# Linear attention and a Strassen feed-forward block: score products as 64x64 quarters, regrouped attention stages, and a fixed TensorE order

## The chip, the cores and the metric

The kernel runs on one core of one Trainium2 chip. The metric is the device time of one execution in microseconds (us). Before the change three runs gave 666.48, 668.00 and 668.18 us, with a median of 668.0 us.

A core has a matrix engine (TensorE, "PE" in the profile, with its weight loads listed as "PEld"), VectorE ("DVE"), ScalarE ("ACT"), GpSimd ("POOL") and SyncE ("SP"). Each engine works through its own queue of instructions in order, and waits at the head of it on semaphores of the others. DMAs are started here from the queues of SP and POOL. TensorE reads SBUF and writes PSUM, which has 8 banks of 128x512 floats.

## The reference

```
# lightning attention, per batch entry and head, blocks of 64 rows, state starts at 0
intra = (q_b k_b^T * lam^(i-j) for i >= j) v_b
inter = (q_b * lam^(i+1)) state
out_b = intra + inter
state = lam^64 * state + (k_b * lam^(63-i))^T v_b
# the heads side by side are the rows x (3072 x 512) of the feed-forward block
h = x @ w_in            # 512 x 2048
y = (h - tanh(h)) @ w_out   # 2048 x 512
```

There are 4 batch entries, 8 heads, 768 positions and 64 columns per head. All is in float32. The size of a block is free in the mathematics, and the kernel uses 128 rows.

## The kernel before

**Groups and chunks.** A group `g` (0 to 5) is 128 positions of all four batch entries, 512 rows of `x`. A chunk `(g, b)` is the part of one batch entry. The four chunks of a group are handled as two halves, `(0, 1)` and `(2, 3)`.

**Attention of a chunk.** `att_transpose` brings q and k into the layout with the head columns on partitions (for g of 2 and more with VectorE transposes of tiles `q_blk` and `k_blk`), and multiplies q by the powers of lam (`qd`). `att_scores` makes the scores: 8 matmuls of 64 contraction rows and 128 output partitions, two heads at a time on the two row halves of the array, into two banks `sp`, each of which VectorE multiplies with the decay mask (`ss`). `att_out` adds, per half, the products of the state with `qd` (L400, 64x64 quarters of the array) and of `v` with `ss` (L406, two column halves of 64) in two banks `op`, which ScalarE copies to `xt`. `att_state` decays k on VectorE (`att_decay`, L361), makes the products of k and v (L374, bank `kv`, two column halves) and updates the state with two VectorE instructions (L379, L380). `att_sums` then makes the sums of `xt` that the feed-forward block needs.

**Feed-forward.** Both products use Strassen's scheme of seven products, in the form named 1, 2, 6, 5, 7, 3, 4, with sums made by VectorE. The up projection (`up`, L458) goes through four column parts `u`. For g of 2 and more its products 2 and 4 are split a second time (`inner_steps`, L542), and so are most products of the down projection (`down_twice`, L686; a plain one is `down`, L633). A partial product stays in a PSUM bank `y`, is copied by ScalarE after each product that completes a quarter, and the next product is added to it in the same bank.

**PSUM.** Four banks have the tag `att`; the other four, `ya`, `yb`, `z` and `w`, belong to the feed-forward block, one buffer each. The bank `y` of an up projection is `ya` for even `u` and `yb` for odd `u`. Both calls of `inner_steps` use `yb` for their `y` (L542), and the ScalarE copies out of it are L546.

**Order.** While the feed-forward block of group g runs, the attention of group g+1 is laid between its products: transposes of `(0, 1)` in part u=2 of the up projection, their scores in u=3, their output and state after the down product 2; then transposes, scores, and output with state of `(2, 3)` after the twice split down products 4, 5 and 6. After the down projection come the products 3 of group g and `inner_steps` 2 of group g+1 in turn, then `inner_steps` 4 mixed with the first up products. Python code gives this program order, but the scheduler of the framework may exchange instructions of an engine by its own estimate, except where `tc.keep_in_program_order` (or `tied` with a true first argument) forbids it. Most matmuls of the feed-forward block and of the attention for g over 0 are free in this sense.

**Loads.** `k_nat` and `v_nat` tiles (256 KB) and the blocks `q_blk`, `k_blk` are loaded by DMAs from the SP queue in a fixed order; k has 3 buffers, v has 4, and the blocks have 7. The tiles `wb` of the feed-forward weights come through POOL, 7 ahead.

Of the kernel before, what the change touches and what calls it, by code (L numbers as in the profile page):

```python
# [24 lines left out]
def kernel(  # L25
# [91 lines left out]
    lam_blk = fwd[:, :, BLK - 1:BLK][:, None, :, :].to_broadcast([128, 2, NP, D])  # L117

# [8 lines left out]
    def load_natural(g, b, names):  # L127
        for name, src, bufs in (("q", q, 2), ("k", k, 3), ("v", v, 4)):
            if name in names:
                x = (qpool if name == "q" else io).tile([128, H, D], F32, name=f"{name}_nat", tag=name, bufs=bufs)  # L130
                op = nc.sync.dma_start(out=x, in_=src[b, :, ts(g, BLK), :].rearrange("h s d -> s h d"))
                tc.keep_in_program_order(op)
                raw[g, b][name] = x
# [189 lines left out]
    def att_transpose(g, bs):  # L323
        for b in bs:
            load(g * B + b + 1)
            t = raw[g, b]
            qt = work.tile([128, NP, BLK], F32, name="qt", tag="qt")
            kt = work.tile([128, NP, BLK], F32, name="kt", tag="kt")
            for dst, x in ((qt, "q"), (kt, "k")):
                if g >= GB:  # L330
                    tc.keep_in_program_order(nc.vector.transpose(out=dst.rearrange("d p i -> d (p i)"),
                                                                 in_=t[x + "b"].rearrange("d p r a -> d (p r a)")))
                else:
                    tp = bank("tp", "att", 4).rearrange("d (p s) -> d p s", p=NP)
                    for p in range(NP):
                        tied(g == 0 or p == 0, nc.tensor.transpose(out=tp[:, p, :], in_=t[x][:, 2 * p:2 * p + 2, :],
                                                                   identity=ident))
                    tied(g == 0, nc.scalar.activation(dst, tp, AF.Copy))
            qd = None
            if g > 0:  # L340
                qd = work.tile([128, NP, BLK], F32, name="qd", tag="qd")
                nc.vector.tensor_tensor(qd, qt, fwd, op=AL.mult)
            tr[g, b] = (qt, kt, qd)

    def att_scores(g, bs):
        for b in bs:
            qt, kt, _ = tr[g, b]

            sp = [bank("sp", "att", 4).rearrange("s (p i) -> s p i", p=NP) for _ in range(2)]
            for p in range(NP):  # L350
                for j in range(2):
                    tied(g == 0, nc.tensor.matmul(out=sp[j][:, p, :], lhsT=kt[ts(j, 64), p, :],  # L352
                                                  rhs=qt[ts(j, 64), p, :], start=True, stop=True))
            ss = work.tile([128, 2, NP, BLK], F32, name="ss", tag="ss")
            for j in range(2):
                tied(g == 0, nc.vector.tensor_tensor(ss[:, j], sp[j], mask[:, j], op=AL.mult))  # L356
            sc[g, b] = ss
# [4 lines left out]

    def att_state(g, bs):
        if g == NG - 1:
            return

        kv = bank("kv", "att", 4).rearrange("d (b p e) -> d b p e", b=2, p=NP)
        for n, b in enumerate(bs):
            kd, vn = raw[g, b]["k"], raw[g, b]["v"]
            if g > 0:  # L370
                att_decay(g, b)
            for p in range(NP):
                for j in range(2):
                    tied(g == 0, nc.tensor.matmul(out=kv[ts(j, 64), n, p, :], lhsT=kd[:, 2 * p + j, :],  # L374
                                                  rhs=vn[:, 2 * p + j, :], start=n == 0 and p == 0, stop=True,
                                                  skip_group_check=True))
        st = state[:, bs[0]:bs[0] + 2]
        if g > 0:
            nc.vector.tensor_tensor(st, st, lam_blk, op=AL.mult)  # L379
            nc.vector.tensor_tensor(st, st, kv, op=AL.add)  # L380
        else:
            tied(True, nc.scalar.activation(st, kv, AF.Copy))

    def att_out(g, bs):
# [3 lines left out]
        ops = [bank("op", "att", 4).rearrange("d (p b s) -> d p b s", p=2, b=2) for _ in range(2)]  # L388
# [5 lines left out]
        if g > 0:  # L394
            for n, b in enumerate(bs):
                for p in (0, 1):
                    for j in range(2):
                        r = ts(j, 64)
                        for pp in (p, p + 2):
                            nc.tensor.matmul(out=dst(n, pp, j), lhsT=state[r, b, pp, :], rhs=tr[g, b][2][r, pp, :],  # L400
                                             start=n == 0 and p == 0, stop=False, skip_group_check=True)
        for n, b in enumerate(bs):
            ss, vn = sc.pop((g, b)), raw[g, b]["v"]
            for p in range(NP):
                for j in range(2):
                    tied(g == 0, nc.tensor.matmul(out=dst(n, p, j), lhsT=vn[:, 2 * p + j, :], rhs=ss[:, j, p, :],  # L406
# [42 lines left out]
    def up(g, u, n):  # L449
# [6 lines left out]
        for m in range(2):  # L456
            for kt in range(2):
                nc.tensor.matmul(out=t[:, m, :], lhsT=wt[:, kt, ts(m, 128)], rhs=x[:, kt, :],  # L458
                                 start=first and m == 0 and kt == 0, stop=kt == 1, skip_group_check=True)
# [4 lines left out]
        def finish(c, src):  # L464
            th = work.tile([128, 2, HB], F32, name="th", tag="th")
            nc.scalar.activation(th, src, AF.Tanh)  # L466
# [6 lines left out]
        elif g >= GI and n == 5:  # L473
            nc.scalar.activation(dst(22), z, AF.Copy)
# [10 lines left out]
        elif n == 6:  # L485
            nc.scalar.activation(dst(12), y, AF.Copy)
# [43 lines left out]
    def inner_steps(g, n, tag):  # L530
# [4 lines left out]
        for x in STEPS:  # L535
# [3 lines left out]
            for u in range(NU):  # L539
                a = wb.rearrange("p m c -> p (m c)")[:, ts(u, 128)] if wb is not None else a_quarter(  # L540
                    n, u, *{1: (0, 0), 2: (0, 1), 7: (1, 0), 4: (1, 1)}[x])
                nc.tensor.matmul(out=dst[:, ts(u, 128)], lhsT=a, rhs=b, start=x in (1, 2, 5) and u == 0, stop=True,  # L542
                                 skip_group_check=True)
            d = dst.rearrange("q (u c) -> q u c", u=NU)
            if x in (1, 4, 6):
                nc.scalar.activation({1: c11, 4: c21, 6: c12}[x], d, AF.Copy)  # L546
            elif x == 5:
                nc.scalar.activation(r5, dst, AF.Copy)
# [73 lines left out]
    def down(g, n):  # L622
# [6 lines left out]
        for u in range(NU):  # L629
            wb = piece(g, n, u)  # L630
            for m in range(2):
                for kt in range(2):
                    nc.tensor.matmul(out=t[:, m, :], lhsT=a[:, u, kt, ts(m, 128)], rhs=wb[:, kt, :],  # L633
                                     start=first and u == 0 and m == 0 and kt == 0, stop=u == NU - 1 and kt == 1,
                                     skip_group_check=True)
# [3 lines left out]
        if n == 1:  # L639
            res[g, 1] = otile("q1")  # L640
            nc.scalar.activation(res[g, 1], t, AF.Copy)
        elif n == 4:
            res[g, 4] = otile("q4")
            nc.scalar.activation(res[g, 4], t, AF.Copy)
# [30 lines left out]
    def down_twice(g, n, zw):  # L675
# [5 lines left out]
        for x, a, dst, keep in ((1, a11, y, o[:, 0:128]), (2, a12, zw[:, 0:128], None), (6, s2, y, o[:, 128:256]),  # L681
# [3 lines left out]
            for u in range(NU):  # L685
                nc.tensor.matmul(out=dst, lhsT=a[:, u, :], rhs=wb[:, ts(u, 128)], start=x in (1, 2) and u == 0,  # L686
                                 stop=u == NU - 1, skip_group_check=True)
            if keep is not None:
                nc.scalar.activation(keep, dst, AF.Copy)  # L689
# [189 lines left out]
    up(1, 0, 1)  # L879
    for g in range(1, NG):  # L880
        last = g == NG - 1
        p0, p1 = attention(g + 1) if not last else ([], [])
        for u in range(NU):
            for n in (2, 6, 5, 7, 1, 4, 3) if g < GI else (1, 7, 3) if u == 0 else (6, 5, 1, 7, 3) if u + 1 < NU else (
# [7 lines left out]
                if g == 1 and u < 2 and n == 5:  # L892
                    sums_in(u + 2)
            if g == GI - 1:
                inner_weights(u)
            if not last and u > 1:
                run(p0[u - 2:u - 1])
        if twice(g, 4):
            sums_twice(g, 4)
        every(down(g, 2))  # L900
        run(p0[2:])
        sums_twice(g, 5)
        every(down_twice(g, 4, "z") if twice(g, 4) else down(g, 4))
        run(p1[0:1])
        sums_once(g, 21, 21, 11)
        sums_twice(g, 6)
        every(down_twice(g, 5, "w"))
        run(p1[1:2])
# [5 lines left out]
        run(p1[2:])  # L914
# [12 lines left out]
        for n in (None, None, 1, None, None, 6, None, None, 5, None):  # L927
            if n is None:
                next(p4)
            else:  # L930
                up(g + 1, 0, n)
        every(p4)
# [30 lines left out]
```

## Time and profile before

| | |
|---|---|
| median of three runs | 668.0 us (666.48 to 668.18) |
| time of the profiled execution | 667.48 us |
| its span from the first to the last instruction | 665.7 us |
| TensorE busy | 653.7 us, 98% |
| VectorE busy | 480.1 us, 72% |
| ScalarE busy | 214.8 us, 32% |
| GpSimd busy | 196.4 us, 30% |
| mean granted TensorE clock | 1.000 |

A float32 matmul leaves two records on TensorE, so a product of 4 matmuls is listed as x8. In a timeline, the first column is the start of a run of like instructions, the second is the time from the start of its first to the end of its last one. Since matmuls are pipelined, the end lies some 0.17 to 0.27 us behind the point at which the next one starts, and the cost of a run is best read as the difference of two starts.

### The profile page before, as it was taken

The page shows a single profiled execution, that of the slowest core. Times are in us where ns is not written, and L with a number is a line of the kernel's source. Part 1 is how long each engine was busy: PE and PEld are TensorE (multiplying, and loading weights), DVE is VectorE, ACT ScalarE, POOL GpSimd, SP SyncE. Part 2 cuts the span into 40 slices and gives each one's busy share as a digit, 9 for nine tenths or more (in the row PEclk, how much of TensorE's full clock was granted, in tenths as well). Part 3 has the DMA queues.
Part 4 walks back from the last instruction along what each step waited for, and adds up shares of the span by engine and source line. Part 5 has one row for each costly group of instructions (what it writes and reads, how often), then busy time and mean ns, then how long its engine had stood idle before and what let it go on. Part 6 is the DMA issues. An engine that isn't in the chain of part 4 may idle for free.

```text
span 665.7 us, 13244 instructions
## 1 busy us (share of the span) xinstructions
PE 653.7 (98%) x4992; PEld 594.6 (89%) x4992; DVE 480.1 (72%) x869; ACT 214.8 (32%) x413; POOL 196.4 (30%) x340
## 2 busy tenths in 40 slices
PE   8899999999999999999999999999999999999988
PEld 7788888888888999888999988999988899988987
DVE  4468897997778983489895378896378787357743
ACT  4788923423321113341112343112333112334110
POOL 0001415783122444001435101345200255300351
PEclk9999999999999999999999999999999999999999
DMA  9999936997345979426889533798721677600584
GB/s 215 226 205 272 294 124 221 347 323 215 79 91 147 294 219 268 88 52 133 233 236 288 132 73 87 182 291 252 202 50 37 156 239 237 205 16 1 141 278 167
DMA packets 158959, 121.76 MB, mean 183 GB/s; under 512 B 133872, under 2 KB 135024, under 8 KB 158896
## 3 DMA queue, kind: packets, MB, share of 16 engines
q0 software_dynamic: 26400, 86.27, 40.7%
q1 hardware_dynamic: 132352, 34.64, 25.6%
q8 instruction: 40, 0.66, 0.4%
q14 instruction: 23, 0.19, 0.1%
q10 hardware_dynamic: 144, 0.00, 0.0%
HBM read 100.67 MB, written 20.19 MB: 182 GB/s over the span
## 4 chain that ended last, share of the span: by engine, by line
PE 76%; issue 9%; DVE 5%; DMA 5%; POOL 2%; ACT 2%; SPq 1%; POOLq 0%; DVEq 0%; ACTq 0%
PE y L458 14%; PE y L686 11%; PE z L458 8%; PE zw L686 8%; PE h L741 7%; PE w L633 4%; PE y L633 4%; PE y L542 3%; PE sp L352 3%; PE op L406 3%; PE acc L771 2%; PE z L542 2%; PE op L400 1%; PE end L725 1%; DMA fine<-wt 1%
## 5 line engine op out<-in xcount | busy, mean ns | idle before, releaser
L598 POOL DMA_DIRECT2D wb<-fine x168 | 90.8, 540 | 138.0 <-PE y L686 59.8
L466 ACT ACTIVATE th<-g 128x512 f32<-128x512 f32 x76 | 47.6, 630 | 99.6 <-DVE g L471 34.2
L689 ACT ACTIVATE q<-y 128x128 f32<-128x128 f32 x96 | 26.7, 278 | 150.3 <-PE y L686 149.5
L458 PE MATMUL y<-xt,w 128*128 128x256 f32 x320 | 73.5, 380 | 0.0
L601 POOL DMA_DIRECT2D wb<-factors x44 | 23.9, 544 | 165.1 <-PE y L633 127.8
L458 PEld LDWEIGHTS y<-xt,w 128*128 128x128 f32 x320 | 59.9, 190 | 8.5 <-ACT g L546 0.9
L467 DVE TENSOR_TENSOR g<-g,th 128x512 f32<-128x512 f32 x76 | 52.1, 689 | 21.1 <-ACT th L466 21.0
L686 PE MATMUL y<-wb,g 128*128 128x128 f32 x456 | 60.6, 278 | 0.0
L741 PE MATMUL h<-xt,w 128*128 128x256 f32 x256 | 58.0, 383 | 1.5 <-DVE w L296 1.4
L686 PEld LDWEIGHTS y<-wb,g 128*128 128x128 f32 x456 | 55.1, 192 | 1.3 <-issue 0.3
L741 PEld LDWEIGHTS h<-xt,w 128*128 128x128 f32 x256 | 47.7, 190 | 9.4 <-DVE w L296 2.1
L686 PE MATMUL zw<-wb,g 128*128 128x128 f32 x304 | 40.3, 275 | 0.1
L458 PE MATMUL z<-tt,ws 128*128 128x256 f32 x160 | 38.1, 381 | 0.0
L458 PE MATMUL y<-tt,ws 128*128 128x256 f32 x160 | 37.8, 379 | 0.0
L458 PE MATMUL z<-xt,ws 128*128 128x256 f32 x160 | 37.8, 379 | 0.0
L686 PEld LDWEIGHTS zw<-wb,g 128*128 128x128 f32 x304 | 37.0, 192 | 0.2 <-DVE g L691 0.2
L633 PE MATMUL w<-wb,g 128*128 128x256 f32 x160 | 35.8, 382 | 0.0
L633 PE MATMUL y<-wb,g 128*128 128x256 f32 x160 | 35.4, 379 | 0.0
L356 DVE TENSOR_TENSOR ss<-sp,mask 128x512 f32<-128x512 f32 x48 | 31.1, 683 | 5.8 <-PE sp L352 5.8
L633 PEld LDWEIGHTS y<-wb,g 128*128 128x128 f32 x160 | 30.4, 190 | 4.1
L458 PEld LDWEIGHTS z<-xt,ws 128*128 128x128 f32 x160 | 30.4, 190 | 4.1
L633 PEld LDWEIGHTS w<-wb,g 128*128 128x128 f32 x160 | 30.1, 190 | 4.4
(178 smaller groups left out, 1292.9 us busy)
## 6 DMA issues: line engine op xcount, KB each, us to landing
wb<-fine POOLq DMA_DIRECT2D x168, 256.0 KB, 4.0
wb<-factors POOLq DMA_DIRECT2D x44, 256.0 KB, 4.3
v_nat<-in_v_dram SPq DMA_DIRECT2D x24, 256.0 KB, 4.8
wb<-fine_in POOLq DMA_DIRECT2D x24, 256.0 KB, 4.3
k_nat<-in_k_dram SPq DMA_DIRECT2D x20, 256.0 KB, 4.9
raw<-in_moe_w_out_dram POOLq DMA_DIRECT2D x10, 512.0 KB, 4.9
raw<-in_moe_w_in_dram SPq DMA_DIRECT2D x8, 512.0 KB, 5.7
raw<-in_moe_w_in_dram SPq DMA_DIRECT2D x16, 256.0 KB, 5.9
```

Of the source, the lines that this page charges most:

```text
L352: tied(g == 0, nc.tensor.matmul(out=sp[j][:, p, :], lhsT=kt[ts(j, 64), p, :], rhs=qt[ts(j, 64), p, :], start=True, stop=True))
L356: tied(g == 0, nc.vector.tensor_tensor(ss[:, j], sp[j], mask[:, j], op=AL.mult))
L458: nc.tensor.matmul(out=t[:, m, :], lhsT=wt[:, kt, ts(m, 128)], rhs=x[:, kt, :], start=first and m == 0 and kt == 0, stop=kt == 1, skip_gro ...
L466: nc.scalar.activation(th, src, AF.Tanh)
L467: nc.vector.tensor_tensor(dst(c), src, th, op=AL.subtract)
L542: nc.tensor.matmul(out=dst[:, ts(u, 128)], lhsT=a, rhs=b, start=x in (1, 2, 5) and u == 0, stop=True, skip_group_check=True)
L598: nc.gpsimd.dma_start(out=t.rearrange("p m c -> p (m c)"), in_=fine[TWICE.index(n_), SUB.index(x_)].rearrange("p u c -> p (u c)"))
L601: nc.gpsimd.dma_start(out=t, in_=factors[XAT[FACT[n_][1]]][:, 2 * x_:2 * x_ + 2, :])
L633: nc.tensor.matmul(out=t[:, m, :], lhsT=a[:, u, kt, ts(m, 128)], rhs=wb[:, kt, :], start=first and u == 0 and m == 0 and kt == 0, stop=u = ...
L686: nc.tensor.matmul(out=dst, lhsT=a[:, u, :], rhs=wb[:, ts(u, 128)], start=x in (1, 2) and u == 0, stop=u == NU - 1, skip_group_check=True)
L689: nc.scalar.activation(keep, dst, AF.Copy)
L741: tied(u == 0, nc.tensor.matmul(out=hm[c][:, m, :], lhsT=w1[u][:, i, a, ts(m, 128)], rhs=xt[0, t][:, i, :], start=m == 0 and i == 0, stop= ...
```

## The change

Nine things change, all for the attention of g from 2 on unless another group is named, and for the order of instructions:

1. The score matmuls are cut into two output halves, so that each one is a 64x64 quarter of the array (L352 before, L359 after): 16 matmuls a chunk instead of 8.
2. The transposes of chunks `(0, 1)` of group g+2 are made while group g+1 starts its up projection; those of `(2, 3)` of g+1 at the end of part u=3. Their scores follow in this order: those of `(0, 1)` at the end of u=2, those of `(2, 3)` after the down product 2, directly ahead of the output of `(0, 1)`. The attention of group 2, which runs beside group 1, keeps the old places for transposes and scores.
3. The output of `(2, 3)` and the state products of all four chunks follow after the twice split down product 6.
4. The output of `(0, 1)` uses the banks `yb` and `w` for groups over 2.
5. The decay of k goes from VectorE (one 128x512 instruction a chunk) to ScalarE (8 instructions of 128x64 a chunk, `decay_steps`), placed between the feed-forward products.
6. The state update is one `scalar_tensor_tensor` for each pair of heads (four of 128x128 a half) instead of two instructions of 128x512 a half; this holds from group 1 on.
7. `qd` of `(2, 3)` is made after the output of `(0, 1)` for groups over 2.
8. The k tile of chunk 3 has a buffer of its own (`k4`).
9. Nearly all matmuls, and most ScalarE copies, are kept in program order.

```diff
+                if name == "k" and b == 3 and g >= GB:
+                    x = late["pool"].tile([128, H, D], F32, name="k_nat", tag="k4", bufs=1)
...
-            qd = None
-            if g > 0:
-                qd = work.tile([128, NP, BLK], F32, name="qd", tag="qd")
-                nc.vector.tensor_tensor(qd, qt, fwd, op=AL.mult)
-            tr[g, b] = (qt, kt, qd)
+            tr[g, b] = (qt, kt)
+            if g > 0 and (g <= GB or b < 2):
+                att_query(g, (b,))
...
+            part = 64 if g >= GB else 128
             for p in range(NP):
                 for j in range(2):
-                    tied(g == 0, nc.tensor.matmul(out=sp[j][:, p, :], lhsT=kt[ts(j, 64), p, :],
-                                                  rhs=qt[ts(j, 64), p, :], start=True, stop=True))
+                    for r in range(128 // part):
+                        tied(g != 1, nc.tensor.matmul(out=sp[j][ts(r, part), p, :], lhsT=kt[ts(j, 64), p, ts(r, part)],
+                                                      rhs=qt[ts(j, 64), p, :], start=True, stop=True))
...
+    def decay_steps(g, b):
+        x = raw[g, b]["k"]
+        for h in range(H):
+            tied(True, nc.scalar.activation(x[:, h, :], x[:, h, :], AF.Copy, scale=mask[:, h % 2, h // 2, BLK - 1:BLK]))
+            yield
...
-            nc.vector.tensor_tensor(st, st, lam_blk, op=AL.mult)
-            nc.vector.tensor_tensor(st, st, kv, op=AL.add)
+            for p in range(NP):
+                nc.vector.scalar_tensor_tensor(out=st[:, :, p, :], in0=st[:, :, p, :], scalar=fwd[:, p, BLK - 1:BLK],
+                                               in1=kv[:, :, p, :], op0=AL.mult, op1=AL.add)
...
-        ops = [bank("op", "att", 4).rearrange("d (p b s) -> d p b s", p=2, b=2) for _ in range(2)]
+        tags = (("yb", 1), ("w", 1)) if g > GB and half == 0 else (("att", 4),) * 2
+        ops = [bank("op", *tag).rearrange("d (p b s) -> d p b s", p=2, b=2) for tag in tags]
...
# up (and likewise down, down_twice, inner_steps; their ScalarE copies are tied too)
-                nc.tensor.matmul(out=t[:, m, :], lhsT=wt[:, kt, ts(m, 128)], rhs=x[:, kt, :],
-                                 start=first and m == 0 and kt == 0, stop=kt == 1, skip_group_check=True)
+                tc.keep_in_program_order(nc.tensor.matmul(
+                    out=t[:, m, :], lhsT=wt[:, kt, ts(m, 128)], rhs=x[:, kt, :],
+                    start=first and m == 0 and kt == 0, stop=kt == 1, skip_group_check=True))
...
# the loop over g
-            if not last and u > 1:
+            if not last and g == 1 and u > 1:
                 run(p0[u - 2:u - 1])
+            if not last and g > 1 and u == 2:
+                att_scores(g + 1, (0, 1))
+            if not last and g > 1 and u == 3:
+                att_transpose(g + 1, (2, 3))
+            if g + 2 < NG and u == (1 if g > 1 else 2):
+                fading = (x for b in (0, 1) for x in decay_steps(g + 1, b))
...
         every(down(g, 2))
-        run(p0[2:])
+        if not last:
+            if g > 1:
+                att_scores(g + 1, (2, 3))
+            att_out(g + 1, (0, 1))
+            if g > 1:
+                att_query(g + 1, (2, 3))
...
         every(down_twice(g, 6, "z"))
...
-        run(p1[2:])
+        if not last:
+            att_out(g + 1, (2, 3))
+            att_state(g + 1, (0, 1))
+            att_state(g + 1, (2, 3))
+            att_sums(g + 1, None)
         every(down_twice(g, 7, "w") if twice(g, 7) else down(g, 7))
...
                 up(g + 1, 0, n)
+                if g + 2 < NG and n in (1, 6):
+                    att_transpose(g + 2, (n // 6,))
```

## The prediction

> **What bounds the kernel now.** I read the page first, then the timeline of TensorE in one attention stage and in the stretch from one group to the next, then ScalarE and VectorE beside it, and the waits.
>
> ```profile
> span 665.7 us, 13244 instructions
> PE 653.7 (98%) x4992; PEld 594.6 (89%) x4992; DVE 480.1 (72%) x869; ACT 214.8 (32%) x413; POOL 196.4 (30%) x340
> ```
>
> TensorE sets the time. What counts is the start of each of its runs, and only a change of its work, or a wait in its queue, moves the end. An attention half of group 3, on TensorE:
>
> ```profile
> 306.73 1.89 PE L458 MATMUL z<-xt,ws 128*128 128x256 f32 x8
> 308.55 2.06 PE L352 MATMUL sp<-qt,kt 64*128 64x128 f32 x32
> 310.53 7.17 PE L633 MATMUL w<-wb,g 128*128 128x256 f32 x32
> 317.63 1.10 PE L400 MATMUL op<-qd,state 64*64 64x128 f32 x32
> 318.67 1.97 PE L406 MATMUL op<-ss,v_nat 128*64 128x128 f32 x32
> 320.47 1.10 PE L374 MATMUL kv<-v_nat,k_nat 128*64 128x64 f32 x32
> 321.50 1.16 PE L686 MATMUL y<-wb,g 128*128 128x128 f32 x8
> 322.49 1.06 PE L686 MATMUL zw<-wb,g 128*128 128x128 f32 x8
> 323.38 1.06 PE L686 MATMUL y<-wb,s 128*128 128x128 f32 x8
> ```
>
> Differences of starts give the prices. A product L686 costs 0.89 (322.49 to 323.38), 0.11 per full-array record of 128 columns. At each change of the array's form some 0.1 is lost on both sides: L458 before the scores takes 1.82 where such a run takes 1.73 elsewhere; the scores take 1.98, where 32 records in pairs would take 1.79; L633 takes 7.10 instead of 6.91 (as in the chain of waits); L400 takes 1.04, where 32 records in fours would take 0.89; the first L686 takes 0.99.
>
> The stretch to the next group, on TensorE and then on ScalarE:
>
> ```profile
> 364.58 1.06 PE L542 MATMUL y<-tt,w 128*128 128x128 f32 x8
> 365.48 1.06 PE L542 MATMUL w<-tt,w 128*128 128x128 f32 x8
> 366.37 1.11 PE L542 MATMUL y<-tt,w 128*128 128x128 f32 x8
> 367.32 1.89 PE L458 MATMUL y<-xt,w 128*128 128x256 f32 x8
> ...
> 376.08 1.05 PE L542 MATMUL y<-tt,w 128*128 128x128 f32 x8
> 376.97 3.71 PE L458 MATMUL y<-xt,w 128*128 128x256 f32 x16
> 380.51 1.89 PE L458 MATMUL z<-xt,ws 128*128 128x256 f32 x8
> ```
>
> ```profile
> 365.68 0.60 ACT L546 ACTIVATE g<-y 128x512 f32<-128x512 f32 x1 [0.62 <-PE y L542]
> 367.52 0.60 ACT L546 ACTIVATE g<-y 128x512 f32<-128x512 f32 x1 [1.25 <-PE y L542]
> ...
> 376.28 0.60 ACT L474 ACTIVATE g<-z 128x512 f32<-128x512 f32 x1 [2.92 <-PE z L458]
> 377.17 0.60 ACT L546 ACTIVATE g<-y 128x512 f32<-128x512 f32 x1 [0.29 <-PE y L542]
> ```
>
> The y at 364.58 ends `inner_steps` 2 and the y at 366.37 begins `inner_steps` 4; both use the one bank `yb`. The second may start only when ScalarE has copied the first (365.68 to 366.28), and it starts 0.09 later. The scheduler had laid the w product, which needs no such copy, between them, so almost nothing was lost. The same at 376.08: the last y of `inner_steps` 4 leaves `yb` at 377.77, and the first product for u=1, which writes `yb` too, is the wait in this line:
>
> ```profile
> PEld y L458 <- ACT g L546: 0.9, 4, 0.2
> ```
>
> It is only 0.2 in each of four groups, because the run x16 at 376.97 begins with two matmuls (four records, 0.86) of product 7 of u=0, which use `ya`.
>
> **The change part by part.** The order of the instructions on each engine is fixed in the built kernel, and I read it there.
>
> *Two inversions on TensorE.* With the attention left out, the order differs from before in exactly two places, in each of the four passages from group 1 to 2 up to 4 to 5, because program order is now binding. First, `inner_steps` 4 begins with its y (product 1) and has the w (product 2) behind it. The y must wait for the copy that ends at 366.28, so it starts near 366.35 instead of 365.48. In front of it nothing is left to do, and everything on TensorE is queued behind it. It takes 0.99 rather than 0.89, since the weight load behind a wait lies open (as at 321.50), and w 0.89 more: the next product starts at 368.23 instead of 367.32, a loss of 0.91. Second, the four matmuls of product 1 of u=1 now come directly after the last y of `inner_steps` 4, and those of product 7 behind them. They wait until 377.77 plus 0.05, where TensorE would go on at 376.97: 0.85. (The 0.09 by which the x16 run, 3.54, exceeds twice 1.73 stays.) Later, at 383.96, before has a run of 1.79 for 1.73, a wait for VectorE's sum out of z, that the delay covers: −0.06. Together 1.70 a passage, times 4: +6.8.
>
> *Scores as quarters, and fewer changes of form.* A stretch of scores is 64 records in fours, priced as two L400 runs with one switch (2×1.04−0.15=1.93) against 1.98. The switches of a group before are, per half, 0.09+0.19 (scores), 0.19 (L633, both sides), 0.15 (L400), 0.14 (kv, whose 32 records in pairs of half length would take 0.89 of 1.03) and 0.10: 0.86, twice 1.72. After, scores of `(0, 1)` alone: 0.09+0.15+0.10=0.34; scores of `(2, 3)`, then L400 in the same form, then L406: 0.09+0.15+0.14+0.10=0.48; output of `(2, 3)` and all state products: 0.48. Sum 1.30, so 0.42 less in each of groups 3, 4 and 5. With 0.05 for each of 8 stretches of scores (groups 2 to 5): −1.7. The lower bound is 0 for the quarters, if they ran only as fast as the pairs: −1.3.
>
> *State products together.* The records are the same; only their place differs. The update is 8 VectorE instructions of 128x128 a group instead of 4 of 128x512. Nothing in the trace does this operation. A 128x128 L525 takes 0.29 alone and starts every 0.20 in a row; that form is nearest, and I take 0.20. The dearer end is 0.42, a 128x256 L696. The eight lie ahead of L691 of down product 7, whose third product by my reckoning waits for nothing for another 0.8. At 0.42 they cost 8×0.22−0.8, about 1.0 in each of three groups: +3.0, kept for the range.
>
> *VectorE in front of the third zw of down product 4.* This is the tight place. From the last tanh subtraction (310.10) VectorE now has in a row: four sums with that subtraction (2.40), four transposes (2.44, as at 328.02 before), nine instructions of 0.60 (5.41), two `qd` (1.14), four score masks (2.41): L691 starts at 323.90, ends at 324.59. TensorE reaches the matmuls that read its result at 324.70 on the same clock. It just misses or just makes it: between 0 and 0.3, taken as 0.12, three groups: +0.36. Before, the same wait came in down product 5 (0.02 with 0.10 for an open weight load) and is gone there, since the transposes left that place: −0.36. In group 1 the decays (2×0.60) and state update (2×0.60) leave VectorE ahead of the late L691 at 219.54, which cost 0.32: −0.3.
>
> *Decay on ScalarE.* 96 instructions of 128x64. Between 128x128 (0.28) and the line through 128x512 (0.59) lies 0.23: 22 us on an engine that is busy for 215 of 666. Behind each stand copies of y in ScalarE's queue, but two fit in the 1.5 that it idles between two copies (L689: "1.51 <-PE y L686"), and a full-array product lies between a copy and the next writer. Zero; without that idle time each would cost up to 0.28.
>
> *Transposes moved into the passage.* Six VectorE instructions, 3.58, run ahead of the sum (L550) that frees y for the last product of `inner_steps` 4. It then starts near 375.7 on the delayed clock instead of 374.6 and TensorE wants y at 377.0. Zero, with 0.5 to spare.
>
> *Banks and loads.* `w` is read by L657 until 316.8, and the output wants it at 317.3; `yb` is long free. POOL's queue is the same instruction for instruction. SP's has the same DMAs in the same order; the extra k buffer lets those behind chunk 3's tile go earlier in group 1, into its down projection. Block loads ran beside the down products before (after the transposes at 328 to 331) without a stall of TensorE. Zero.
>
> Sum against the profiled execution, 667.5 (span 665.7 and 1.8 around it; 0.5 under the median): +6.8−1.7+0.36−0.36−0.3=+4.8, so **672.3**.
>
> **The rivals.**
>
> *Faster: the copies do not hold TensorE.* If TensorE went on with the w product, or with product 7, past the waiting y, the 6.8 vanishes and so do 0.15 a passage paid now: 667.5−1.7−0.3−0.6=664.9. For it: only the bank and not the data stands in the way. Against: the 0.2 waits above, and at 227.41 a zw waited 0.8 for VectorE (L691) and nothing passed it. It decides below a loss of 0.5 a passage. 6%.
>
> *Only one of the two binds* (a copy sooner than read): 672.3−3.5=668.8. Against: both copies start where their product ends. 8%.
>
> *Heavier: VectorE.* The update at 0.42, L691 late by 0.3 instead of 0.12: 672.3+3.0+0.5=675.8. 10%.
>
> *TensorE's instruction supply becomes the bound.* The stretches of short matmuls grow from 96 records (L400, L406, L374: 3.87, 0.040 each) to 128. If 0.040 were the limit, 128 records would take 5.15 where the array needs 4.67; six stretches: +2.9, 675.2. Against: L374's 32 come last in theirs and still take only 0.032 each. 5%.
> The Trainium skill ("TensorE: Matmul & The Clock Gate", section "Wait — 56ns, not 53.3ns?") states a cost of about 62 ns of the sequencer per matmul in one of its decode modes, the bound where the array's work is shorter. By that the 128 records would take 7.9, the estimate would be 19 higher, near 692; the 0.040 of this trace speaks against it.
>
> **How the numbers follow.** My forecast has 71%, within 671 to 674. Under 668.8 lie the faster case and half of the single wait; the heavy ends reach 676. The DMA wait of 1.9 near the end (the chain's "DMA wb<-fine", 6.63 against a median of 4.0) may come out shorter, which also lowers it. So the range is 668.8 to 676.0. A difference under 0.3%, 2.0 us, can't be told from none here: slower holds the forecast, the heavier case and the supply bound (86%), same the single wait (8%), faster 6%.
>
> **What would show it.** The changed profile should have waits of TensorE (y of L542 and L458) for the L546 copies of about 0.8 each, four of either kind; scores of 64 records in 1.93; no gap between scores of `(2, 3)` and L400; VectorE near 470, ScalarE near 237; a wait of 0.1 at most in down product 4. It is wrong if those y waits are near zero, if quarters take well over 1.98, or if the update takes over 0.4 a piece.

## The result, and the profile after

The changed kernel takes 678.61 us (median of five runs, 676.24 to 678.82). The kernel before, run beside it, took 668.0 us (666.48 to 668.18). The ratio is 1.0154, with a 95% interval of 1.0131 to 1.0177. The change costs 10.6 us. The forecast was 4.8 us more than the profiled execution of before, 672.3, with a range up to 676.0: the direction was right, and the size was less than half of what came.

The profiled execution of the changed kernel took 676.7 us. Its page:

```profile
span 674.5 us, 13882 instructions
PE 654.0 (97%) x5248; PEld 594.4 (88%) x5248; DVE 471.1 (70%) x873; ACT 237.7 (35%) x509; POOL 196.2 (29%) x340
```

TensorE's busy time is the same as before (654.0 and 653.7) while the span grew by 8.8: the loss is waiting. VectorE and ScalarE have the loads that were forecast, 471 and 238. What TensorE and its weight loads waited for, from the view of waits (in total, how often, the longest):

```profile
PE y L475 <- ACT g L565: 2.7, 4, 0.7
PE y L560 <- ACT g L565: 2.7, 4, 0.7
...
PE y L706 <- DMA wb<-fine: 1.9, 3, 0.9
PE zw L706 <- DMA wb<-fine: 1.5, 2, 1.3
...
PE z L560 <- DMA wb<-fine_in: 0.8, 1, 0.8
...
PEld y L560 <- ACT g L565: 3.5, 4, 0.9
PEld y L475 <- ACT g L565: 3.5, 4, 0.9
```

The waits for the copies L565 (L546 before) are the two inversions, four of each kind. Of the waits for `wb`, the one of 1.3 stands near the end, where the kernel before has one of 1.7; the others were not in the forecast. The passage from group 1 to 2 on TensorE:

```profile
261.64 1.06 PE L560 MATMUL y<-tt,w 128*128 128x128 f32 x8
263.38 1.16 PE L560 MATMUL y<-tt,w 128*128 128x128 f32 x8 [0.69 <-ACT g L565]
264.37 1.06 PE L560 MATMUL w<-tt,w 128*128 128x128 f32 x8
265.27 1.89 PE L475 MATMUL y<-xt,w 128*128 128x256 f32 x8
...
274.02 1.05 PE L560 MATMUL y<-tt,w 128*128 128x128 f32 x8
275.76 1.56 PE L475 MATMUL y<-xt,w 128*128 128x256 f32 x6 [0.69 <-ACT g L565]
```

From the first y to the product behind w are 3.63 us, where the same three runs took 2.74 before (364.58 to 367.32 in the prediction's lines), and from the y at 274.02 to the next product are 1.74 instead of 0.89. These are losses of 0.89 and 0.85, for which 0.91 and 0.85 were forecast.

An attention stage, now scores of `(2, 3)`, then the output of `(0, 1)`, in group 2's down projection:

```profile
314.23 7.07 PE L652 MATMUL w<-wb,g 128*128 128x256 f32 x32
321.23 1.98 PE L359 MATMUL sp<-qt,kt 64*64 64x128 f32 x64
323.03 1.05 PE L416 MATMUL op<-qd,state 64*64 64x128 f32 x32
324.01 1.97 PE L423 MATMUL op<-ss,v_nat 128*64 128x128 f32 x32
325.91 1.16 PE L706 MATMUL y<-wb,g 128*128 128x128 f32 x8
```

The 128 short records take 4.68 us, as against 4.67 that the forecast gave them, with no gap between the scores and L416.

To see where the rest came from, I cut both traces at the first product of each down projection and at the first `inner_steps` run of each passage, and compared the lengths of the stretches (us, after minus before):

| stretch | group 1 | 2 | 3 | 4 | 5 |
|---|---|---|---|---|---|
| from the first `inner_steps` ahead of the group to its down projection (passage and up) | | +3.80 | +3.80 | +4.81 | +1.69 |
| its down projection, to the next `inner_steps` or the end | +1.77 | -2.58 | -2.58 | -2.04 | -0.10 |

The last passage has no attention beside it and shows the inversions alone: 1.69. In groups 2 and 3 the rest of the change gives 3.80-1.69-2.58 = -0.47 each, close to the forecast (0.42 for changes of form, 0.10 for quarters). What doesn't fit is +1.77 in group 1 where a small gain was expected, and 1.0 more in the passage ahead of group 4 with 0.5 more in that group's down projection.

In group 1 TensorE waits for weights in down product 5:

```profile
220.16 1.06 PE L706 MATMUL y<-wb,g 128*128 128x128 f32 x8
222.15 1.16 PE L706 MATMUL y<-wb,gS 128*128 128x128 f32 x8 [0.94 <-DMA wb<-fine]
...
224.86 1.13 PE L706 MATMUL y<-wb,s 128*128 128x128 f32 x8 [0.64 <-DMA wb<-fine]
226.20 1.16 PE L706 MATMUL zw<-wb,s 128*128 128x128 f32 x8 [0.21 <-DMA wb<-fine]
```

Those weights come from POOL's queue. There, in the changed kernel, the loads stop for five microseconds behind the store of `o11`:

```profile
212.13 0.54 POOL L617 DMA_DIRECT2D wb<-fine  x1 [0.33 <-PE w L652]
217.24 0.72 POOL L629 DMA_DIRECT2D out_dram<-o  x1 [4.57 <-issue]
217.96 3.20 POOL L617 DMA_DIRECT2D wb<-fine  x6
```

and in the kernel before, the same instructions in the same order:

```profile
212.00 0.54 POOL L598 DMA_DIRECT2D wb<-fine  x1 [0.40 <-PE w L633]
215.71 0.72 POOL L610 DMA_DIRECT2D out_dram<-o  x1 [3.17 <-DVE g L620]
216.97 0.56 POOL L598 DMA_DIRECT2D wb<-fine  x1 [0.54 <-PE y L686]
217.84 0.54 POOL L598 DMA_DIRECT2D wb<-fine  x1 [0.32 <-PE zw L686]
```

The store waits for VectorE's sum of `o11`, and it starts 1.50 us after that sum ends in both kernels. On VectorE the sum has moved. Changed kernel:

```profile
212.53 0.68 DVE L690 TENSOR_TENSOR s<-gS 128x512 f32<-128x512 f32 x1
213.14 0.68 DVE L639 TENSOR_TENSOR g<-g,g 128x512 f32<-128x512 f32 x1
214.45 0.69 DVE L691 TENSOR_TENSOR s<-s,gS 128x512 f32<-128x512 f32 x1 [0.63 <-DMA fine_in<-ws]
215.06 0.68 DVE L677 TENSOR_TENSOR o<-q,w 128x512 f32<-128x512 f32 x1
```

Kernel before:

```profile
212.32 1.29 DVE L361 TENSOR_TENSOR k_nat<-k_nat,mask 128x512 f32<-128x512 f32 x2
213.53 0.68 DVE L657 TENSOR_TENSOR o<-q,w 128x512 f32<-128x512 f32 x1
```

VectorE's instructions are still free, and the scheduler now puts three sums for later products ahead of the sum of `o11`. One of them waits 0.63 for a DMA. So the sum ends at 215.74 instead of 214.21. TensorE, meanwhile, reaches product 4 at 214.70 instead of 215.49, since the state products stand elsewhere. The first load behind the store was issued 1.48 us after the start of product 4 before, and is issued 3.26 us after it now.

### The profile page after: what moved, and what is told of

It reads as the page before. It is cut to its first block, busy times and chain, and to the rows that moved or that the text cites. A ratio compares the mean times of both kernels' runs of the same rounds, so it can differ in the third digit from the quotient of the medians.

```text
span 674.5 us, 13882 instructions
## 1 busy us (share of the span) xinstructions
PE 654.0 (97%) x5248; PEld 594.4 (88%) x5248; DVE 471.1 (70%) x873; ACT 237.7 (35%) x509; POOL 196.2 (29%) x340
```

## The experiments

Each ratio is to the kernel before, run beside the experiment on the same chip; there its median was 666.7 for the first four, 667.3 for the next four and 667.2 for the last three. The diffs are shortened.

### Both copies covered

In the changed kernel, `inner_steps` 4 has its w product ahead of its first y again, and product 7 of u=0 stands ahead of product 1 of u=1. All else is as changed.

```diff
             # inner_steps
+            for x_ in {1: (2, 1), 2: ()}.get(x, (x,)) if n == 4 else (x,):
                 for u in range(NU):
...
-            for n in ... else (1, 7, 3) if u == 0 else ...
+            for n in ... else (7, 1, 3) if u == 0 else ...
```

> The changed kernel with two products moved on TensorE and nothing else: in inner_steps 4 the w product goes ahead of the first y, and in the up projection's part 0 (groups 2 to 5) product 7 goes ahead of product 1 of the next part. Theory A (each passage loses 0.95 and 0.85 to the copies out of yb, and nothing else hangs on them): both waits vanish, with the 0.09 that was left even before, so 4 x 1.85 = 7.4 less than the changed kernel's 678.6, near 671.2, about 3 over the kernel before. Rival B (VectorE or ScalarE are late in the passage anyway, because six instructions were put ahead of the sum that frees y): the time moves to the last y of inner_steps 4, and less than 4 of the 7.4 comes back, 675 or more.

Measured: 669.48 us, ratio 1.0041 (1.0024 to 1.0057). All eight waits for L565 are gone; the last passage is 0.15 shorter than in the kernel before. So the inversions hold 1.1% of the time, some 7.5 us. It also shows that the rest of the change, by itself, costs 2.7 us, where the forecast had a gain of 2.0, or of 2.6 with the 0.15 that each passage of the kernel before still pays. Group 1's down projection was 59.42 us here (56.84 before).

### The order alone

The kernel before, with the feed-forward matmuls bound to program order and nothing else changed.

```diff
-                nc.tensor.matmul(out=t[:, m, :], ...)
+                tc.keep_in_program_order(nc.tensor.matmul(out=t[:, m, :], ...))
...  # likewise in inner_steps, down and down_twice
```

> The kernel before with only the order of the feed-forward matmuls bound to program order; attention, loads, ScalarE and VectorE work as before. Theory A: the two waits of each passage come with it, 4 x 1.71 = 6.8 more than the kernel before, near 674.8, that is most of the loss with none of the regrouping. Rival B (the loss comes from the regrouping, and the order matters little): within 2 us of the kernel before.

Measured: 673.99 us, ratio 1.0107 (1.0091 to 1.0123), 7.1 us. The same two waits, four of each:

```profile
PEld y L543 <- ACT g L548: 3.5, 4, 0.9
PEld y L458 <- ACT g L548: 3.5, 4, 0.9
```

Three of the stretches of passage and up projection grew by 1.69, and the one ahead of group 4 by 1.92. This settles the first step of the forecast (6.8): it is right. The question left is the other 2.7.

### The store behind the loads

In the changed kernel, the store of `o11` of group 1 goes behind the seven loads for down product 5 in POOL's queue. These loads and the store are also bound to program order.

```diff
-            store(g, 11, o11)
+            if g == 1: late["o11"] = o11      # stored after the loads for product 5
+            else: store(g, 11, o11)
```

> The changed kernel with one DMA moved: in group 1 the store of the result o11 goes behind the seven loads of the weights for down product 5 in POOL's queue, instead of ahead of them. Theory A (in group 1 the store stands at the head of POOL's queue until 217.2 and waits for VectorE, so the weights of product 5 are sent late and TensorE waits 3 us for them between 220 and 230): these waits go, 2 to 3 us less than the changed kernel, near 676. Rival B (the weights are late because the block loads of group 3 now run in this place on the same DMA engines): the waits stay and the time is that of the changed kernel within 0.5.

Measured: 677.61 us, ratio 1.0158 (1.0126 to 1.0191): no gain. TensorE still waits for `wb` in product 5, and I first took this as the end of the theory of the store. The timelines of POOL and then of TensorE say otherwise:

```profile
212.60 0.54 POOL L617 DMA_DIRECT2D wb<-fine  x1 [0.32 <-PE w L653]
217.82 2.12 POOL L617 DMA_DIRECT2D wb<-fine  x4 [4.69 <-PE zw L710]
```

```profile
215.16 1.16 PE L710 MATMUL y<-wb,g 128*128 128x128 f32 x8
```

The product that frees the load's buffer ends at 216.32, and the load starts at 217.82: 1.50 us later, although nothing stands ahead of it. (The row names the zw product behind it, 216.15 to 217.21. By the order of the buffers, and by the row at 216.97 of the kernel before, it is y that frees this load; the trace alone doesn't tell the two apart.) In the kernel before, a load starts 0.32 after such a product (215.49+1.16 to 216.97). It seems that the first DMA that POOL issues at this place of its program is 1.50 late, be it the store or a load. In the kernel before, the store takes this delay while TensorE is still in the state products. In this experiment the first load takes it, so that only 0.6 of the 1.8 us is won back (2.66 after the start of product 4, instead of 3.26). By this reading the move was a wrong test: it took the store away and left the delay.

### Both

The edits of "Both copies covered" and "The store behind the loads" together.

> The two edits before together. Theory A: they are independent, so 7.4 and 2.5 less than the changed kernel, near 668.7, equal to the kernel before within what can be told. If it lies 2 us or more above the kernel before, something else in the regrouped attention costs time, such as the loads of k, v and the blocks at their new places. By the count of switches of the array's form alone (1.7 less) it would be near 666.

Measured: 667.25 us, ratio 1.0009 (0.9989 to 1.0029). Group 1's down projection was 57.46 here, 2.0 shorter than with the copies covered alone; the intervals of the two ratios overlap a little.

### The sum of `o11` in its old place

If the delay is there in any case, the sum has to come earlier. Here the copies are covered, and VectorE makes the sum of `o11` of group 1 ahead of the three sums that had passed it. No other instruction changes its place, on any engine.

```diff
-            nc.vector.tensor_tensor(o11, res[g, 1], t, op=AL.add)
+            late["sum"] = nc.vector.tensor_tensor(o11, res[g, 1], t, op=AL.add).ins
...
-        sums_twice(g, 5)
+        with tc.issue_after(late["sum"]):   # for g == 1; likewise sums_once(g, 21, 21, 11)
+            sums_twice(g, 5)
```

> Both copies of the passage covered, as in e1_covered, and in group 1 VectorE makes the o11 sum (L677) three instructions earlier, ahead of the sums for product 5; no other instruction moves on any engine. Theory A (the store of o11 stands at the head of POOL's queue until its sum is made, and the weight loads behind it come late): the sum ends 1.8 us earlier, the store goes near 215.5 instead of 217.6 and the first load behind it near 216.5 instead of 218.3, TensorE has no wait for wb in the down products 4 and 5 of group 1, and group 1's down projection is 2.0 to 2.6 us shorter than in e1_covered (59.4 from its first product to the first inner_steps). In all 667.0, a ratio to before of 0.998 to 1.000. Theory B (the transfers themselves take longer, because SP's block loads run beside them, wherever the store stands): waits for wb stay at 2 us or more and the ratio at 1.003 to 1.005.

Measured: 666.96 us, ratio 0.9990 (0.9969 to 1.0011), 0.5% less than with the copies covered alone. POOL's queue:

```profile
214.09 0.72 POOL L629 DMA_DIRECT2D out_dram<-o  x1 [2.04 <-DVE s L690]
215.55 0.55 POOL L617 DMA_DIRECT2D wb<-fine  x1 [0.74 <-PE y L706]
```

The loads follow TensorE's products again. Group 1's down projection is 56.80 us, 2.62 shorter. One wait of 0.81 for `wb` stays at 225.23, so "no wait" was too much to expect; the expected length of the stretch and the expected ratio held. This speaks against theory B, since SP's loads keep their place.

### The same in the changed kernel

The sum of `o11` moved in the same way, the copies left uncovered.

> The changed kernel with the same VectorE instruction moved (o11 sum of group 1 three instructions earlier), the passages left as they are. Theory A: 2.0 us less than the changed kernel, a ratio to before of 1.0125 instead of 1.0155, no waits for wb in group 1's products 4 and 5. Theory B: 1.0155.

Measured: 674.75 us, ratio 1.0100 (1.0077 to 1.0123), against 1.0154 (1.0131 to 1.0177) without: 3.6 us less, and the intervals lie apart. Group 1's down projection is 56.50 us instead of 58.62, and product 5 has no wait over 0.4.

### The sum late in the kernel before

The reverse: in the kernel before, the sum of `o11` of group 1 goes behind four other VectorE instructions, its store with it. The sum and the one ahead of it are bound to program order.

```diff
         nc.vector.tensor_tensor(s2, s1, a11, op=AL.subtract)
+        if (g, n) == (1, 5):                       # was in down(1, 2)
+            nc.vector.tensor_tensor(o11, q1, t, op=AL.add)
+            store(g, 11, o11)
```

> The kernel before with one VectorE instruction of group 1 put back: the o11 sum (L657 of before) behind the first two sums for product 5 and the state decay, four instructions later, its store behind it; all else stands. Theory A: the sum ends near 216.6 instead of 214.2, the store goes near 218.1, the first load behind it near 218.8 instead of 217.0, and TensorE waits for wb in product 5: group 1's down projection (56.8 from its first product to the first inner_steps) grows by 1.3 to 2.2 us, in all 668.5, a ratio of 1.002 to 1.003. Theory B: no change, 1.000.

Measured: 668.27 us, ratio 1.0014 (0.9998 to 1.0031). The profile shows the wait that the changed kernel has, in the same place:

```profile
218.59 0.72 POOL L610 DMA_DIRECT2D out_dram<-o  x1 [5.58 <-issue]
219.30 2.67 POOL L598 DMA_DIRECT2D wb<-fine  x5
```

and on TensorE:

```profile
221.75 1.06 PE L693 MATMUL y<-wb,g 128*128 128x128 f32 x8
224.94 2.02 PE L693 MATMUL y<-wb,gS 128*128 128x128 f32 x8 [2.13 <-DMA wb<-fine]
```

In this execution group 1's down projection is 60.00 us, 3.16 longer than before. The median shows 0.9, with an interval that just reaches no change, so the size differs from execution to execution. Put side by side, the eight kernels with an early first load (1.47 to 1.61 after the start of product 4) have stretches of 56.50 to 57.38, the five with a late one (2.66 to 3.34) have 57.46 to 60.00. The lateness alone doesn't fix the length: at 2.66 it is 57.46 once and 58.39 once. (Times in us, from one profiled execution each; the kernels with quarters, halves and the v tiles late follow below.)

| kernel | sum of `o11` ends | product 4 starts | next `wb` load | after the start of product 4 | group 1's down projection |
|---|---|---|---|---|---|
| before | 214.21 | 215.49 | 216.97 | 1.48 | 56.84 |
| order alone | 214.28 | 215.56 | 217.04 | 1.48 | 57.26 |
| changed, sum first | 211.32 | 212.80 | 214.28 | 1.47 | 56.50 |
| covered, sum first | 212.59 | 214.07 | 215.55 | 1.47 | 56.80 |
| quarters alone | 215.34 | 215.95 | 217.56 | 1.61 | 56.77 |
| quarters alone, sum kept | 214.38 | 215.59 | 217.07 | 1.48 | 56.83 |
| covered, sum first, v tiles late | 215.37 | 216.86 | 218.33 | 1.47 | 57.11 |
| covered, sum first, halves | 213.24 | 214.81 | 216.28 | 1.47 | 57.38 |
| both (covered, store late) | 218.47 | 217.45 | 220.11 | 2.66 | 57.46 |
| changed, store late | 216.38 | 215.16 | 217.82 | 2.66 | 58.39 |
| changed | 215.74 | 214.70 | 217.96 | 3.26 | 58.62 |
| covered | 216.12 | 215.08 | 218.33 | 3.25 | 59.42 |
| before, sum late | 217.09 | 215.97 | 219.30 | 3.34 | 60.00 |

### Quarters alone

The kernel before with the scores of groups 2 to 5 as quarters.

```diff
-                    tied(g == 0, nc.tensor.matmul(out=sp[j][:, p, :], lhsT=kt[ts(j, 64), p, :], ...))
+                    for r in range(2 if g >= GB else 1):   # half = ts(r, 64) for g >= GB, else all
+                        tied(g == 0, nc.tensor.matmul(out=sp[j][half, p, :], lhsT=kt[ts(j, 64), p, half], ...))
```

> The kernel before with the score matmuls of groups 2 to 5 cut into 64x64 quarters and nothing else in the program; VectorE's o11 sum of group 1 comes one instruction later for it. As predicted: 64 records in 1.93 instead of 32 in 1.98, eight stretches, 0.4 less: a ratio of 0.999 to 1.000. Rival (quarters are limited by the number of matmuls and cost more): 2.5 or more for a stretch, 4 us in all, 1.006. Theory A adds under 0.2 in group 1, since the store would go near 216.3, still ahead of the first free buffer at 216.7.

Measured: 668.74 us, ratio 1.0026 (1.0010 to 1.0042), where a gain of 0.4 was forecast. The stretch itself does what was forecast, 1.91 us for 64 records (the next run starts at 231.83):

```profile
229.92 1.98 PE L354 MATMUL sp<-qt,kt 64*64 64x128 f32 x64
```

In this kernel the scheduler lets one sum pass that of `o11`, so the first load comes 1.61 instead of 1.48 after product 4 starts. The next run takes this away.

### Quarters alone, the sum of `o11` kept

The same, with the sum of `o11` bound to its old place.

> As e5_quarters_alone, but the o11 sum of group 1 stands on VectorE where the kernel before has it (behind it, one sum and the state decay change places). Theory A (e5's 1.7 us come from the o11 sum one instruction later, the store at 216.8 and the loads behind it at 217.6): the store goes near 216.2, the first load near 217.4 on e5's clock, and the ratio is that of the quarters alone, 0.999 to 1.000. Theory C (the quarters themselves cost, in a place that the stretches of scores do not show): 1.002 to 1.004 as in e5.

Measured: 668.20 us, ratio 1.0013 (0.9996 to 1.0029), between what the two theories gave. The intervals of the two runs overlap, so the later sum isn't shown to be the cause of 1.0026. In the profiles, both kernels with quarters alone have the same wait, in down product 5 of group 3, which the kernel before hasn't. Here it is without the sum kept:

```profile
435.55 1.13 PE L688 MATMUL y<-wb,s 128*128 128x128 f32 x8 [0.59 <-DMA wb<-fine]
```

With the sum kept it is 0.71. Group 3's down projection is 0.80 and 0.71 us longer than before, while that of group 4 is 0.15 and 0.14 shorter, a little more than the 0.10 forecast. The loads of `wb` issued between 422 and 437 take 5.3 and 5.5 us to land, in the median, as against 4.2 before. So part of what the quarters seem to cost is a later landing of weights; why it is later isn't shown.

### Halves in the regrouped kernel

Copies covered and the sum first, as above, with the scores as 128-row halves again (`part = 128`).

> e7_sum_first with the scores as 128-row halves again (32 records a stretch instead of 64), every other instruction in its place. As predicted of the quarters: 1.98 instead of 1.93 for a stretch and one change of form more ahead of the state products of chunks 0 and 1 (0.15) in three groups, 0.4 plus 0.5, so 0.9 more than e7_sum_first: a ratio of 1.0000 to 1.0005. Theory C (quarters cost 1 to 2 us somewhere else): 0.997 to 0.998.

Measured: 667.02 us, ratio 0.9991 (0.9976 to 1.0006), the same as with quarters (0.9990). The quarters neither gain nor lose anything here that these runs can tell.

### The v tiles of the last group

The loss of 1.0 in the passage ahead of group 4 is a wait for a load. In the changed kernel, SP issues the v tiles of chunks 0 and 1 of the last group in that passage (SP's timeline):

```profile
463.61 1.04 SPq L132 DMA_DIRECT2D v_nat<-in_v_dram  x2
```

In the kernel before they follow in the up projection:

```profile
490.71 1.06 SPq L131 DMA_DIRECT2D v_nat<-in_v_dram  x2
```

The DMAs issued from 457 on, in the changed kernel (20 us) and then in the kernel before (15 us); the last column is the median time from issue to landing:

```profile
wb<-fine_in POOLq DMA_DIRECT2D x6, 256.0 KB, 5.8
...
v_nat<-in_v_dram SPq DMA_DIRECT2D x2, 256.0 KB, 6.8
```

```profile
wb<-fine_in POOLq DMA_DIRECT2D x5, 256.0 KB, 4.4
```

The experiment takes the kernel with copies covered and the sum first, and loads these v tiles behind the last k blocks.

```diff
-            for b in (0, 1): load_natural(g, b, nat)        # ahead of load_blocks(g, 3, "k")
+            for b in (0, 1): if g < NG - 1: load_natural(g, b, nat)
             load_blocks(g, 3, "k")
-            for b in (2, 3): load_natural(g, b, nat)
+            for b in (2, 3) if g < NG - 1 else range(B): load_natural(g, b, nat)
```

> e7_sum_first with the v tiles of chunks 0 and 1 of the last group loaded behind the last k blocks instead of ahead of them; nothing else moves. In the changed kernel these two tiles of 256 KB are issued in the passage from group 3 to 4 (461.4 in e1_covered), the wb<-fine_in loads beside them take 5.9 us instead of 4.4 and TensorE waits 0.8 to 1.0 for one of them in four of six profiles. Theory D (they take the bandwidth there): no wait of z<-xt,wb near 470, latency of wb<-fine_in in that passage back near 4.5, 0.5 to 1.0 less on average than e7_sum_first: a ratio of 0.998. Otherwise: the wait appears as often as before, 0.999.

Measured: 666.48 us, ratio 0.9983 (0.9967 to 0.9999). In the passage TensorE has no wait for a load, and the loads take

```profile
wb<-fine_in POOLq DMA_DIRECT2D x6, 256.0 KB, 3.8
```

The Trainium skill ("DMA: Bandwidth & Descriptors", section "Issuing engines are not separate DMA queues") says that DMAs run on the same 16 engines and interleave, whichever engine started them. The trace agrees: two tiles from SP's queue go with a rise of POOL's loads from 4.4 to 5.8 us. Over all profiles (median landing of these loads between 455 and 477), the seven kernels that issue the two v tiles in this passage have 4.6 to 5.8 us, the three that don't have 3.8 to 4.5. TensorE waits for one of the loads where they take 5.3 or more (0.21 to 0.84, five kernels), and not where they take 4.9 or less. But the kernel that was edited here, with copies covered and the sum first, is one of the latter (4.9): in its profile there is no such wait to lose. So the v tiles are linked with slower loads, and that they caused the loss of 1.0 in the changed kernel is likely but not shown. The gain over the kernel without this edit (0.9990) is smaller than the intervals. This kernel has the lowest ratio of all, 0.2% under the kernel before, with an interval that ends just short of no change.

## Why the prediction was wrong in size

*Two inversions on TensorE (+6.8): right,* in mechanism and size. The order alone costs 7.1 us; covering both copies returns 7.5; each passage lost 1.69 where 1.70 was forecast. The rivals "the copies do not hold TensorE" and "only one binds" are out, since all eight waits are there.

*Quarters and fewer changes of form (-1.7): right in the stages, not seen in the time.* -0.47 a group in groups 2 and 3 against -0.52; 1.91 for a stretch alone against 1.93; 4.68 for the 128 records against 4.67. The supply of instructions isn't a bound: the 64 records of scores in front of L416 take 0.028 each. The 62 ns per matmul of the section that the prediction cites from the Trainium skill ("TensorE: Matmul & The Clock Gate", section "Wait — 56ns, not 53.3ns?") would give the 128 records 7.9 us, an estimate; the trace has 4.68. Counted per matmul of the program, which leaves two records, the same figure would give the 32 matmuls of the scores 1.98, and the trace has 1.80 (321.23 to 323.03). Yet quarters by themselves gave ratios of 1.0026 and 1.0013 instead of 0.9994. The profiles show 0.7 to 0.8 us of this as a wait for late weights in group 3; the cause of that, and the rest, stay open. In the regrouped kernel, quarters and halves take the same time.

*The tight place in down product 4 (+0.36) and its pair in product 5 (-0.36): right in groups 2 and 3.* In group 2 TensorE lost 0.15 there (329.59 to 331.53 is 1.94 for 1.79) against 0.12. In group 4's down projection product 5 lost 0.5 instead of gaining (549.31 to 550.71 is 1.40 for 0.89). The profile puts 0.34 of it down to VectorE's sum L691, but in group 3 the same product starts (443.04) before that sum ends (443.48), so the cause of this wait stays open.

*State products and updates (0): right.* The eight updates take 0.26 each, between the 0.20 taken and the 0.42 kept for the range, and nothing waits behind them. *Decay on ScalarE and transposes in the passage (0): right* too: the decays start 0.23 apart, as taken, and ScalarE's busy time grew by 22.9 where 22 were forecast.

*"In group 1 ... -0.3" and "Banks and loads ... Zero": these steps failed.* I read that VectorE is freed of the decays and the update in group 1, and took the gain. That is what happened at the late L691. But I went by the amount of VectorE's work in front of one instruction and didn't look at what else changed its place there. The sum of `o11` moved back by three sums, and POOL's queue, "the same instruction for instruction", has that sum's store at its head. A queue that holds the same instructions isn't the same queue when its head is released 1.5 us later and its reader comes 0.8 us sooner. Moving that one sum back gave 2.62 us of the stretch in one pair of profiles, 2.12 in the other, and 3.4 and 3.6 us in the medians; moving it in the kernel before made the same wait. The same step also put SP's DMAs at nothing. It looked at group 1 and not at the passage ahead of group 4, where TensorE lost 1.0 to a load of weights in the profiled execution, beside v tiles that SP now issues there; that these are the cause is likely and not shown.

*The sum.* In the profiled executions, the span grew by 8.8: 6.8 from the inversions, 1.8 from group 1 (forecast: a gain of 0.3 and some 0.1 of quarters), -0.9 from the regrouping in groups 2 and 3, +1.1 in group 4 (a gain of 0.5 less a wait of 1.0 and some 0.5 in the down projection), and 0.1 elsewhere. The remaining difference to 10.6 is 0.4 outside the span (2.2 instead of 1.8) and 1.4 because the profiled execution of the changed kernel lies 1.9 under its median and that of before 0.5 under its own. So of the 6.3 us by which 678.6 exceeds 672.3, the late store holds 2.2 in the profiles (3.4 to 3.6 in the medians, by the two kernels with the sum first), and group 4 holds 1.6, whose causes are open. With the copies covered, the sum first and the v tiles late, the forecast's other steps should give 2.6 us less than before (1.7, 0.3, and 0.15 in each passage); measured is 1.1, with an interval of 0.1 to 2.2. In the three kernels with the copies covered and the sum first, a wait of 0.6 for `wb` stands in product 5 of group 2, which isn't explained.

## What to carry to other kernels

Binding an order takes away the scheduler's small repairs: before it is bound, look at every pair of products that share a bank with a copy between them, and write work between them by hand. When instructions of a free engine are added or removed, compare the whole order of that engine, and follow each instruction that moved to what its result releases: the head of a DMA queue above all, since everything behind it waits too. And a test that moves the suspect out of a queue must also show when the next instruction went; moving the store behind the loads nearly cleared the right suspect.

## What was not expected of the hardware

At one place of POOL's program, after 2.0 to 5.6 us without an issue, the first DMA starts 1.50 us after its release, where most others start 0.3 after theirs. It is there in every kernel run here, whether the first one is the store (1.50 after the sum of `o11`, in eleven of the thirteen) or a load (1.50 after the product that is taken to free it, in the two with the store late). The cause wasn't looked for.

Once, with the copies covered and the sum first, TensorE stood for 1.13 us in the middle of the state products, for nothing that the profile shows:

```profile
450.96 1.27 PE L388 MATMUL kv<-v_nat,k_nat 128*64 128x64 f32 x36 [1.13 <-issue]
```

It didn't appear in any other profile.
